# A memory-augmented attention block with a gated MLP on one core: beta loaded behind the transposing loads of the second x segment, its gating instructions moved behind it

## The chip, the cores and the metric

The kernel runs on one core of one Trainium2 chip. Its engines are TensorE (PE: matmuls; PEld: its weight loads), VectorE (DVE), ScalarE (ACT), GpSimd (POOL) and SyncE (SP), which issues most DMAs. The metric is the device time of one execution in microseconds, as the median of several runs; lower is better.

## The reference

The input x is 2048 tokens of 512 bf16 values. Two branches are computed from it and mixed per token by a sigmoid gate.

```python
x = A_x
g = _sigmoid((x * gate_w).sum(-1, keepdims=True))
a = _A_ref(x, A_wq, A_wk, A_wv, A_wo, A_beta)
b = _B_ref(x, B_w_gate, B_w_up, B_w_down)      # (gelu(x@w_gate) * (x@w_up)) @ w_down
return g * a + (1 - g) * b
```

Branch A is attention with 32 heads of width 16 in four segments of 512 tokens. Within a segment it is causal softmax attention; over the segments before, a linear memory (M, z) is read and then updated:

```python
g = _sigmoid(beta).reshape(1, H, 1, 1)
...
a_dot = jnp.einsum('bhqk,bhkd->bhqd', p, vs)
pq = phi(qs)
num = jnp.einsum('bhld,bhde->bhle', pq, M)
den = jnp.einsum('bhld,bhd->bhl', pq, z)[..., None] + 1e-06
o = g * (num / den) + (1.0 - g) * a_dot
```

So beta, 32 values, sets for each head how much comes from the memory and how much from the softmax.

## The kernel before

All work is cut into named tasks, each a short list of instructions on one engine. A long string, ORDER, written out by hand, lists every task once; walking through it, the program appends each task's instructions to its engine's queue. An engine works its queue strictly in that order. Semaphore waits are added where a task reads what another engine wrote, or writes what another engine still reads. The relative order of two tasks on different engines in the string has no effect of its own; the order of two tasks on one engine has.

A name carries the segment and the part. For segment 0: K0_t, Q0_t, V0_m are the projections, G0_f and U0_f the gate and up products of the MLP (14 tiles of 128 columns each), out0_q and wo0_q the output products, all on TensorE. Kev, Qev, Vev, Gev are the evictions of their PSUM results, on DVE or on ACT (`:d` or `:a` behind the name). TensorE's results go to four PSUM banks; the digit behind a TensorE task is the bank. A task that opens a bank waits until the eviction of the bank's former result is done.

The attention scores go a separate way. The four matmul groups of `st0_tA` to `st0_tE` (t is a group of 8 heads) fill a PSUM region of 2048 columns; `exp0_tX` on ACT turns it into one of ten probability tiles, pt; `msk0_tX` on GpSimd multiplies the blocks on the diagonal by a triangle, one instruction per block (one for A, two each for B to E). `pv0_1` on TensorE then takes the probabilities of head groups 0 and 1 times the values, group 0 first, key block by key block in the order 0, 1, 7, 2, 6, 3, 5, 4; blocks 1 and 7 lie in the tiles of part B. Each matmul waits for the masks of its own tile. GpSimd's queue has the masks of groups 0 and 1 in the order 0B, 0D, 0C, 0E, goa0, 0A, 1A, 1C, 1D, gfull, 1B. The results of pv are transposed on DVE (`tp0_...`) and scaled with gq (`pvp0_...`); the eviction order on DVE and the opening of banks on TensorE are again ORDER's.

The tasks of beta form a chain across the engines:

```python
one("betab", DVE, ...)   # 4 copies: ball -> betab, one row of 8 values for each of 4 partition groups
one("bexp", ACT, ...)    # gq = exp(betab); gfull = exp(-ball)
one("gqa", POOL, ...)    # gq = gq + 1
one("gqb", DVE, ...)     # gq = 1 / gq      (this is 1 - sigmoid(beta))
one("gfull", POOL, ...)  # gfull = gfull + 1
```

`ld_beta` (line 367) is the load ahead of it: 32 values broadcast to 128 partitions, 8 KB. gq is read by the pvp tasks, gfull by the memory reads from segment 1 on.

SP's queue before begins with: x0_0, wk1, x0_t2, x0_t3, wq0, wq1, gw, beta, wv, wg0 (waits until wq1 has landed), the four transposing loads x1_2, x1_1, x1_3, x1_0 of the second x segment, wu1 (waits for wg0), x2_0 (waits for wu1), then vsh0_21 and further loads.

Of the kernel before, what the change touches and what calls it, by code (L numbers as in the profile page):

```python
# [861 lines left out]
ld_x0_0 ld_wk1 ld_x0_1 warm1:0 ident xtr0_1 xev0_1:d xtr0_0 warm2 xev0_0:d vones0 masks ld_wk0 causal1 gwz ld_x0_t2  # L862
ld_x0_t3 ld_wq0 ld_wq1 ld_gw ld_beta causal0 consts K0_1a:1 K0_3a:2 K0_3b K0_2a:3 K0_0a:0 K0_2b K0_0b K0_1b K0_0c
K0_2c K0_3c K0_1c Kev0_0:d Kev0_2:d kpadb0_0 kpadb0_2 causal kpada0_0 Kev0_3:a Q0_0:0 Qev0_0:a Q0_1:3 st0_0A gwtr:2
Kev0_1:d gwev Q0_3:0 ld_wv ld_wg0 Qev0_1:d V0_1b:1 V0_3a:2 V0_3b:3 exp0_0A Qev0_3:d Vev0_3a:a Vev0_1b:a st0_0B
Vev0_3b:d kpada0_2 kpada0_1 V0_0b:0 V0_1a:2 V0_2a:1 Vev0_0b:d G0_6:3 Gev0_6:d Vev0_1a:d Vev0_2a:d exp0_0B st0_0C
exp0_0C Q0_2:0 G0_2:3 V0_2b:2 ld_x1_2 ld_x1_1 betab ld_x1_3 ld_x1_0 st0_0D Vev0_2b:a exp0_0D Gev0_2:d kpadb0_1
Qev0_2:d phka0_0 V1_2b:1 V0_0a:3 G1_6:2 V1_0b:0 Vev1_2b:d phka0_2 st0_0E Vev0_0a:d Vev1_0b:d G0_1:1 bexp Gev1_6:a
exp0_0E Gev0_1:d Q1_2:3 V1_3b:2 V1_3a:0 kpada0_3 Qev1_2:d Vev1_3a:d phkb0_2 phkc0_2 Vev1_3b:d st0_1A gz0 gqa exp0_1A
gr0 Q1_0:1 V1_0a:3 G1_5:0 Vev1_0a:d gqb Gev1_5:d st0_1B Q1_1:2 K1_0:3 exp0_1B phkb0_0 ld_wu1 ld_x2_0 G0_5:0 Qev1_0:d  # L870
kpadb0_3 vsh0_21 st0_1C exp0_1C Qev1_1:d ld_x2_1 ld_x2_3 ktr0_3 ld_wg1 Gev0_5:d V1_2a:1 K1_3:2 K1_1:0 vsh0_01
Vev1_2a:a vsh0_20 ld_x2_2 ktr0_2 vsh0_00 ld_wd1 st0_1D phkc0_0 Kev1_1:d kpada1_1 G0_4:1 G0_3:0 Gev0_4:d Kev1_0:d
Gev0_3:d Kev1_3:a ld_wd0 ld_wu0 ktr0_1 ktr0_0 vsh1_20 ld_wo V1_1a:2 Vev1_1a:d exp0_1D st0_2A exp0_2A msk0_0B msk0_0D
msk0_0C kpada1_0 msk0_0E goa0 gob0 msk0_0A msk0_1A msk0_1C msk0_1D gfull msk0_1B G0_0:1 Q1_3:3 G1_1:0 Qev1_3:d phqa1_0
st0_2B Gev0_0:d Gev1_1:a pv0_1:2301 exp0_2B tp0_d01 tp0_d00 pvp0_01 Q2_0:3 Qev2_0:d tp0_d11 st0_2C K1_2:2 Kev1_2:d
pvp0_00 tp0_d10 gelu0 G0_8:3 G0_13:1 gd0_13 G0_10:2 G0_11:0 G0_9:1 gd0_8 gd0_10 gd0_9 gd0_11 G0_12:3 G0_7:2 gd0_12
G1_2:1 U0_0:0 gd0_7 Gev1_2:d pvp0_11 h0_0 U0_13:3 U0_10:2 h0_10 Q2_1:1 Qev2_1:d exp0_2C st0_2D mz0:0 U0_7:2 U0_9:1
pvp0_10 h0_13 exp0_2D phqb1_0 st0_2E exp0_2E phka1_0 h0_7 mza0 h0_9 ota0_0 phqa1_2 kpadb1_0 G1_4:3 U0_1:2 h0_1
Gev1_4:a V1_1b:0 st0_3A G1_0:1 U0_5:3 Q2_2:2 exp0_3A Vev1_1b:a Gev1_0:a Qev2_2:a kpadb1_1 st0_3B exp0_3B U0_11:0
U0_4:1 U0_12:2 st0_3C phkb1_0 exp0_3C phqc1_0 kpada1_2 h0_4 h0_5 U0_6:1 U0_2:3 h0_11 h0_12 phqb1_2 h0_2 G1_3:0  # L880
Gev1_3:d h0_6 kpadb1_2 st0_3D phka1_2 U0_3:2 h0_3 U0_8:3 h0_8 Q2_3:0 Qev2_3:d exp0_3D phkb1_2 msk0_2A msk0_2B msk0_2C
msk0_3A msk0_2E msk0_2D msk0_3C goc0 msk0_3B st1_0A msk0_3D pv0_3:1230 exp1_0A st1_0B exp1_0B tp0_d20 tp0_d21 pvp0_20
tp0_d30 ota0_1 pvp0_21 tp0_d31 kpada1_3 out0_1_0:1 out0_1_1 out0_1_2 V2_0a:2 Vev2_0a:d G1_9:3 V2_1b:0 Vev2_1b:d
wev0_1:d st1_0C G1_8:2 G1_10:0 G1_11:1 gelu1 gd1_9 G1_7:3 gd1_8 gd1_10 gd1_7 gd1_11 G1_13:2 gd1_13 G1_12:0 gd1_12
phqc1_2 phkc1_0 mzq0 pvp0_31 pvp0_30 ota0_3 V2_0b:3 Vev2_0b:d ota0_2 V2_1a:1 Vev2_1a:d out0_0_0:2 out0_0_1 out0_0_2
nd1_0:0 ndp1_0 phkc1_2 exp1_0C st1_0D exp1_0D K2_0:3 K2_2:1 wev0_0:d Kev2_0:d Kev2_2:a K2_1:0 st1_0E Kev2_1:d U1_2:2
h1_2 wo0_1:1 nd1_3:3 nd1_1:0 exp1_0E st1_1A ld_x3_2 vsh1_00 vsh2_01 ktr1_1 ktr1_0 oev0_1 ndp1_1 wo0_0:2 oev0_0
kpada2_0 vsh1_21 out0_2_0:1 nd1_2:0 msk1_0C msk1_0A exp1_1A st1_1B exp1_1B msk1_0B gz1 msk1_0E msk1_1A msk1_0D msk1_1B
out0_2_1 wo0_2:2 ndp1_2 st1_1C exp1_1C nd1_5:0 out0_2_2 ndp1_3 wev0_2:a ndp1_5 out0_3_0:3 st1_1D nd1_4:0 out0_3_1
out0_3_2 ktr1_2 dma0 vsh1_01 otr1_3 ndp1_4 otr1_0 oev0_2 phka2_0 msk1_1C wev0_3:d ktr1_3 dma1 vsh2_00 otr1_1 ld_x3_1  # L890
ld_x3_0 ld_x3_3 exp1_1D st1_2A exp1_2A gr1 msk1_1D pv1_1:1023 st1_2B exp1_2B tp1_d01 tp1_d00 kpadb1_3 V2_2b:0
Vev2_2b:d K2_3:1 Kev2_3:a G2_3:0 pvp1_00 Gev2_3:d tp1_d10 st1_2C U1_8:1 G2_1:0 otr1_2 V2_3a:2 h1_8 Gev2_1:d Vev2_3a:d
kpadb2_0 kpadb2_1 exp1_2C st1_2D phkb2_0 exp1_2D G2_6:1 wo0_3:0 U1_3:2 pvp1_01 tp1_d11 Gev2_6:a h1_3 phka2_2 oev0_3
st1_2E U1_0:3 V2_3b:1 G2_0:2 Gev2_0:d h1_0 Vev2_3b:d exp1_2E phkb2_2 st1_3A mz1:0 G2_4:2 G2_5:3 pvp1_10 mza1 Gev2_5:d
exp1_3A st1_3B exp1_3B Gev2_4:d U1_11:1 G2_2:0 Gev2_2:d ota1_0 U1_13:3 h1_13 U1_10:2 h1_10 h1_11 G2_11:0 G2_10:3
pvp1_11 phkc2_0 phkc2_2 ota1_1 otm1_0 otm1_1 G2_12:2 G2_9:1 st1_3C gelu2 gd2_11 gd2_12 G2_7:0 G2_13:2 gd2_10 gd2_9
gd2_7 gd2_13 G2_8:3 gd2_8 U1_7:1 U2_9:0 K3_0:2 h1_7 U2_5:3 Q3_0:1 phqa2_0 h2_9 h2_5 Qev3_0:d Kev3_0:d exp1_3C st1_3D
exp1_3D U1_1:0 U2_12:3 msk1_3A msk1_2A msk1_3B U2_13:1 h2_12 h1_1 h2_13 kpada2_1 st2_0A U1_9:2 V2_2a:3 U2_7:0 msk1_2D
msk1_2B msk1_2E h1_9 Vev2_2a:d vsh2_20 dma2 dma3 ktr2_0 ktr2_2 vsh2_21 exp2_0A phqb2_0 msk1_3D msk1_2C msk1_3C st2_0B
h2_7 kpada2_2 pv1_3:1230 tp1_d21 exp2_0B tp1_d20 V3_1a:2 Vev3_1a:a st2_0C exp2_0C pvp1_21 tp1_d31 U1_6:1 Q3_1:2  # L900
V3_0a:0 st2_0D h1_6 pvp1_20 Vev3_0a:d Qev3_1:a V3_2b:1 U1_4:2 U1_5:0 exp2_0D st2_0E exp2_0E tp1_d30 phqc2_0 h1_5 h1_4
ota1_2 Vev3_2b:a U1_12:3 h1_12 pvp1_31 pvp1_30 out1_1_0:0 st2_1A V3_1b:2 out1_1_1 V3_3a:3 exp2_1A st2_1B msk2_0B
msk2_0D Vev3_3a:a exp2_1B out1_1_2 U2_4:1 msk2_0E goa1 gob1 kpadb2_3 kpada2_3 msk2_0C msk2_0A msk2_1A ota1_3 h2_4
otm1_2 otm1_3 K3_1:3 mzq1 Vev3_1b:a wev1_1:a st2_1C msk2_1B goc1 U2_1:2 Q3_3:1 V3_0b:0 Kev3_1:d kpada3_0 h2_1 Qev3_3:d
kpadb2_2 exp2_1C msk2_1C st2_1D V3_2a:3 U2_6:2 exp2_1D Vev3_2a:a wo1_1:1 Vev3_0b:d kpadb3_0 h2_6 oev1_1 st2_2A msk2_1D
pv2_1:0231 exp2_2A st2_2B exp2_2B tp2_d00 pvp2_00 phqa2_2 tp2_d01 tp2_d10 pvp2_10 pvp2_01 tp2_d11 out1_0_0:0 out1_0_1
st2_2C phqb2_2 out1_0_2 V3_3b:2 Vev3_3b:d wev1_0:d out1_3_0:3 phqc2_2 pvp2_11 exp2_2C st2_2D exp2_2D wo1_0:1 out1_3_1
st2_2E nd2_0:2 out1_2_0:0 out1_3_2 msk2_2C gz2 gr2 gz3 gr3 goa3 ndp2_0 gob3 oev1_0 msk2_2D goc3 goa2 gob2 exp2_2E
st2_3A exp2_3A msk2_3A msk2_2B wev1_3:d G3_4:2 nd2_2:1 out1_2_1 Gev3_4:a ndp2_2 st2_3B exp2_3B nd2_4:3 G3_1:1 Gev3_1:d
out1_2_2 nd2_1:2 st2_3C dma4 ktr2_1 vsh3_20 vsh3_01 ktr2_3 dma5 ndp2_4 ndp2_1 G3_3:1 wo1_3:3 exp2_3C Gev3_3:a K3_2:2  # L910
st2_3D wev1_2:a msk2_2A kpada3_1 oev1_3 Kev3_2:d nd2_5:1 nd2_3:3 G3_0:0 G3_5:2 ndp2_3 ndp2_5 Gev3_0:d msk2_3C msk2_2E
exp2_3D st3_0A exp3_0A goc2 msk2_3D msk2_3B G3_2:3 wo1_2:1 Gev3_2:d G3_6:0 Gev3_6:a Gev3_5:d oev1_2 ota2_0 st3_0B
pv2_3:3210 exp3_0B tp2_d20 tp2_d21 K3_3:3 Kev3_3:a pvp2_20 pvp2_21 U2_3:2 tp2_d30 h2_3 st3_0C U2_8:3 U2_0:1 tp2_d31
otr2_2 otr2_0 dma6 dma7 otr2_1 vsh3_00 otr2_3 vsh3_21 h2_0 ota2_1 G3_7:2 G3_12:0 G3_10:1 gelu3 gd3_7 h2_8 ota2_2
kpadb3_2 kpadb3_3 pvp2_30 pvp2_31 ota2_3 G3_8:3 gd3_10 gd3_12 gd3_8 G3_9:2 G3_11:1 gd3_11 gd3_9 G3_13:0 U2_11:3 Q3_2:1
U2_10:2 Qev3_2:d h2_10 gd3_13 U2_2:0 U3_13:1 exp3_0C st3_0D exp3_0D h2_2 h2_11 otm2_3 otm2_2 kpadb3_1 otm2_0 otm2_1
# [42 lines left out]
```

## Time and profile before

| | |
|---|---|
| runs | 263.14, 263.89, 518.72 us; median 263.89 |
| profiled execution | 264.53 us, of it 262.8 us span |
| TensorE busy | 257.9 us, 98% of the span |
| DVE, ACT, POOL busy | 75%, 77%, 38% |
| granted TensorE clock | 1.00 |
| DMA | 16.50 MB, most of it in the first 46 us |

The three runs are one execution each; the profiled execution is another one. The profile's timeline lists instructions by start, duration, engine, line and operation, with the tile written and the tiles read; `x8` means that neighbours of one kind were merged, and a bracket gives the idle time of the engine ahead of the instruction and what ended it. A line number is often that of a helper shared by many tasks; which task it is follows from its place in ORDER.

### The profile page before, as it was taken

Reading aid. Unit: us, or ns where it says so; the run is one execution under the profiler, and the core shown is the slowest. Engines: PE = TensorE matmul, PEld = TensorE weight load, DVE = VectorE, ACT = ScalarE, POOL = GpSimd, SP = SyncE. Lnnn points to the kernel's source line nnn. Section 1 sums busy time; section 2 is a strip of 40 time slices with the busy share of each in tenths; the row PEclk is TensorE's granted clock in tenths of the full one; section 3 lists DMA queues with packets and bytes.
Section 4 is the critical chain, followed back from the end, with each engine's and each line's share of the span. In section 5 each row is a group of like instructions: output and inputs, shape, how many; then the busy total and the mean of one; then the engine's idle time right before and its main releaser. Section 6 shows DMA issues by size and latency. Waiting matters only on the chain.

```text
span 262.8 us, 6704 instructions
## 1 busy us (share of the span) xinstructions
PE 257.9 (98%) x2849; PEld 122.5 (47%) x2849; DVE 197.4 (75%) x412; ACT 203.2 (77%) x171; POOL 99.1 (38%) x163
## 2 busy tenths in 40 slices
...
GB/s 186 244 160 144 163 278 275 93 2 1 5 28 2 61 43 39 91 75 2 2 0 71 35 0 2 2 41 61 68 79 0 2 1 22 3 0 42 62 42 80
DMA packets 31974, 16.50 MB, mean 63 GB/s; under 512 B 21576, under 2 KB 31944, under 8 KB 31944
## 3 DMA queue, kind: packets, MB, share of 16 engines
...
q8 instruction: 22, 0.36, 0.6%
q10 hardware_dynamic: 416, 0.39, 0.4%
...
## 4 chain that ended last, share of the span: by engine, by line
PE 92%; DMA 4%; SPq 1%; issue 0%; DVE 0%; DVEq 0%
PE psD L448 47%; PE psD L734 19%; PE psX L601 9%; PE psD L643 6%; PE psD L748 5%; PE psD L498 5%; DMA wg<-in_B_w_gate_dram 3%; PE psD L546 1%; DMA wq<-in_A_wq_dram 1%; SPq L361 1%; PE psD L576 1%; SPq L341 1%; DVE ost L752 0%; DVEq L817 0%
## 5 line engine op out<-in xcount | busy, mean ns | idle before, releaser
L608 ACT ACTIVATE pt<-psX 128x2048 bf16<-128x2048 f32 x72 | 135.1, 1877 | 29.5 <-PE psX L601 27.9
L614 POOL TENSOR_TENSOR pt<-pt,ctri 128x256 bf16<-128x256 bf16 x128 | 92.6, 734 | 128.3 <-ACT pt L608 123.8
L448 PE MATMUL psD<-xT,wu 128*128 128x512 bf16 x224 | 54.6, 380 | 0.0
L448 PE MATMUL psD<-xT,wg 128*128 128x512 bf16 x224 | 53.4, 380 | 1.1 <-DMA wg<-in_B_w_gate_dram 1.1
L734 PE MATMUL psD<-wd,gb 128*128 128x512 bf16 x224 | 53.2, 380 | 0.0
L719 DVE TENSOR_TENSOR gb<-psD,gb 128x512 bf16<-128x512 f32 x56 | 37.2, 681 | 10.8 <-PE psD L448 10.7
L448 PEld LDWEIGHTS psD<-xT,wg 128*128 128x128 bf16 x224 | 20.8, 98 | 25.8 <-issue 2.6
L734 PEld LDWEIGHTS psD<-wd,gb 128*128 128x128 bf16 x224 | 20.7, 98 | 24.3 <-issue 2.1
L448 PEld LDWEIGHTS psD<-xT,wu 128*128 128x128 bf16 x224 | 20.2, 98 | 24.7 <-issue 2.6
L601 PE MATMUL psX<-qT,kD 32*128 32x192 bf16 (+7 forms) x512 | 28.5, 287 | 0.0
L529 DVE STREAM_TRANSPOSE tT<-psD 128x512 f32<-128x512 f32 x32 | 21.7, 701 | 5.6 <-PE psD L643 5.1
L442 DVE CAST gb<-psD 128x512 bf16<-128x512 f32 x20 | 13.6, 689 | 13.7 <-PE psD L448 13.7
L601 PEld LDWEIGHTS psX<-qT,kD 32*128 32x128 bf16 x512 | 8.2, 92 | 25.1 <-ACT pt L608 13.4
L498 PE MATMUL psD<-wv,xT 128*128 128x257 bf16 (+1 forms) x128 | 18.2, 273 | 0.0
L752 DVE SCALAR_TENSOR_TENSOR ost<-psD,gtok,wds 128x512 bf16<-128x512 f32 (+1 forms) x17 | 11.9, 711 | 7.7 <-PE psD L748 7.6
L667 DVE SCALAR_TENSOR_TENSOR ob<-tT,gq,rc 128x256 bf16<-128x256 f32 x32 | 16.7, 522 | 1.1
L702 ACT ACTIVATE gb<-psD 128x512 bf16<-128x512 f32 x28 | 15.0, 594 | 3.3 <-PE psD L448 3.3
L643 PE MATMUL psD<-pt,vnat 64*17 64x192 bf16 (+7 forms) x512 | 17.1, 283 | 0.0
L643 PE MATMUL psD<-pt,vsh 64*17 64x192 bf16 (+7 forms) x512 | 17.1, 283 | 0.0
L448 PE MATMUL psD<-xT,wq 128*128 128x512 bf16 x64 | 16.3, 379 | 0.0
L748 PE MATMUL psD<-wo,oT 128*128 128x512 bf16 (+1 forms) x68 | 16.2, 367 | 0.0
L498 PEld LDWEIGHTS psD<-wv,xT 128*128 128x128 bf16 x128 | 11.8, 97 | 6.6 <-issue 1.4
...
## 6 DMA issues: line engine op xcount, KB each, us to landing
...
```

The lines of the kernel that those rows point to most:

```text
L448: one(name, PE, n * T_MM, [I(lambda e, i=i: e.matmul(BK[sl.i][:, :], lhs(i), rhs(i), start=(i == 0), stop=(i == n - 1)), reads(i), [bk(sl) ...
L498: one(f"V{s}_{m}{'ab'[hf]}", PE, 2 * T_MM, [I(lambda e, i=i, sl=sl, a=a, z=z, xs=xs: e.matmul(BK[sl.i][:, 0:z - a], xs(i), wv[:, i, a:z], ...
L529: one(f"tp{name}", DVE, 0.605, [I(lambda e, sl=sl, ti=ti: e.transpose(tT[ti][:, :], BK[sl.i][:, :]), [bk(sl)], [("tT", ti)])], bias=bias)
L601: ins.append(I(lambda e, t=t, kb=kb, ncol=ncol, c0=c0, g=g: e.matmul(XALL[:, g * 512 + c0:g * 512 + c0 + ncol], kD[(4 * s + t) % R_KD][32 ...
L608: one(f"exp{s}_{name}", ACT, 2048 * 0.000833 + 0.05, [I(lambda e: e.activation(pt[slot][:, :, :], xin, ACTF.Exp, scale=ATT_SCALE), [("X",) ...
L614: ins.append(I(lambda e, mv=mv: e.tensor_tensor(mv, mv, cm, ALU.mult), [("pt", slot), ("causal",)], [("pt", slot)]))
L643: ins.append(I(lambda e, kb=kb, slot=slot, c0=c0, n=n, g=g, r0=r0, sl=banks[j], va=va: e.matmul(BK[sl.i][32 * g:32 * g + 17, 64 * kb:512], ...
L667: I(lambda e, ti=ti, ri=ri, t=t, j=j, dst=dst: e.scalar_tensor_tensor(out=dst, in0=t_rows(ti), scalar=gq[:, 2 * t + j:2 * t + j + 1], in1= ...
L702: t = one(f"gd{s}_{ft}", ACT, 0.485, [I(lambda e, gi=gi, f=f, sl=sl: e.activation(gb[gi][:, f, :], BK[sl.i][:, :], ACTF.Gelu_apprx_tanh), ...
L719: one(f"h{s}_{ft}", DVE, 0.605, [I(lambda e, sl=sl, gi=gi, f=f: e.tensor_tensor(gb[gi][:, f, :], BK[sl.i][:, :], gb[gi][:, f, :], ALU.mult ...
L734: mm.append(I(lambda e, fb=fb, gi=gi, f=f, q=q, sl=sl: e.matmul(BK[sl.i][:, :], gb[gi][:, f, q], wd[:, fb, :], start=(fb == 0), stop=(fb = ...
L748: one(f"wo{s}_{qt}{sfx}", PE, 4 * T_MM * w / 512, [I(lambda e, kb=kb, q=q, so=so, c=c, w=w: e.matmul(BK[so.i][:, 0:w], oT[:, kb, q], wo[:, ...
```

## The change

Only the string ORDER is edited; the diff is long because its lines are wrapped anew. It holds the same 1019 words before and after. Five tasks stand elsewhere, with the neighbours that stay:

```diff
 ld_wq1 ld_gw
-ld_beta
 causal0 ...
 V0_2b:2 ld_x1_2 ld_x1_1
-betab
 ld_x1_3 ld_x1_0
+ld_beta
 st0_0D ...
 Vev1_0b:d G0_1:1
-bexp
 Gev1_6:a exp0_0E ...
 st0_1A gz0
-gqa
 exp0_1A gr0 Q1_0:1 V1_0a:3 G1_5:0 Vev1_0a:d
-gqb
 Gev1_5:d st0_1B ... G0_5:0 Qev1_0:d
+betab
 kpadb0_3 vsh0_21 st0_1C exp0_1C
+bexp
 Qev1_1:d
+gqa
 ld_x2_1 ld_x2_3
+gqb
 ktr0_3 ld_wg1 Gev0_5:d V1_2a:1 K1_3:2 K1_1:0 ...
```

Seen by engine: on SP, ld_beta goes from between gw and wv to between x1_0 and wu1. On DVE, betab goes from behind Vev0_2a to behind Qev1_0, and gqb from behind Vev1_0a to behind Qev1_1 and ahead of Gev0_5. On ACT, bexp goes from behind exp0_0D to behind exp0_1C. On GpSimd, gqa stays between gz0 and msk0_0B. TensorE's queue is the same.

More of the change, by code (lines that the diff above doesn't have):

```diff
@@ L861 @@
 ORDER = """
[L862 to L916, printed above, removed]
@@ L917 @@
-h3_13 phqa3_2 out2_1_0:2 out2_1_1 st3_0E exp3_0E mz2:0 U3_7:3 U3_1:1 kpada3_2 mza2 mzq2 h3_1 phqa3_0 h3_7 phqb3_2
-st3_1A U3_9:0 U3_3:1 out2_3_0:3 exp3_1A phqb3_0 h3_3 st3_1B exp3_1B out2_0_0:1 out2_1_2 msk3_0D msk3_0B st3_1C
-out2_0_1 out2_0_2 exp3_1C st3_1D exp3_1D phqc3_2 h3_9 wev2_1:d out2_3_1 wo2_1:0 msk3_0A msk3_1A oev2_1 kpada3_3
-phqc3_0 msk3_0E st3_2A U3_8:2 out2_3_2 U3_6:0 exp3_2A msk3_0C msk3_1C msk3_1B wev2_0:a wev2_3:a msk3_1D h3_8 h3_6
-st3_2B dma9 pv3_1:2130 tp3_d00 tp3_d01 U3_2:2 exp3_2B st3_2C exp3_2C pvp3_00 h3_2 tp3_d10 wo2_3:1 U3_0:2 U3_11:3
@@ L922 @@
-oev2_3 pvp3_01 h3_0 tp3_d11 st3_2D U3_12:1 U3_10:2 h3_11 h3_12 exp3_2D nd3_0:0 ndp3_0 h3_10 st3_2E U3_4:3 wo2_0:1
-nd3_2:0 nd3_1:2 h3_4 exp3_2E st3_3A exp3_3A out2_2_0:3 out2_2_1 st3_3B pvp3_11 ndp3_1 ndp3_2 nd3_3:2 U3_5:0 out2_2_2
-oev2_0 pvp3_10 nd3_5:1 msk3_2B msk3_2A msk3_2D msk3_2E msk3_3A ndp3_3 wev2_2:d h3_5 exp3_3B st3_3C exp3_3C wo2_2:2
-out3_1_0:3 st3_3D out3_1_1 nd3_4:0 out3_1_2 dma8 exp3_3D msk3_3B msk3_2C msk3_3C msk3_3D wev3_1:a ota3_0 ndp3_5 oev2_2
-ndp3_4 ota3_1 dma11 otr3_2 otr3_1 otr3_3 otr3_0 pv3_3:1203 tp3_d20 tp3_d21 pvp3_20 pvp3_21 tp3_d30 tp3_d31 ota3_2
@@ L927 @@
-pvp3_31 pvp3_30 otm3_1 otm3_0 ota3_3 out3_0_0:1 out3_2_0:2 out3_0_1 out3_2_1 out3_3_0:0 out3_0_2 out3_3_1 wev3_0:a
-otm3_2 otm3_3 wo3_0:3 dma10 oev3_0 dma12 wo3_1:1 out3_2_2 out3_3_2 wo3_2:3 oev3_1 wev3_2:a oev3_2 wo3_3b:1 dma13 dma14
-wev3_3:a oev3_3b dma15b wo3_3a:2 oev3_3a dma15a
+ld_x0_0 ld_wk1 ld_x0_1 warm1:0 ident xtr0_1 xev0_1:d xtr0_0 warm2 xev0_0:d vones0 masks ld_wk0 causal1 gwz ld_x0_t2 ld_x0_t3 ld_wq0 ld_wq1 ld_gw
+causal0 consts K0_1a:1 K0_3a:2 K0_3b K0_2a:3 K0_0a:0 K0_2b K0_0b K0_1b K0_0c K0_2c K0_3c K0_1c Kev0_0:d Kev0_2:d kpadb0_0 kpadb0_2 causal kpada0_0
@@ new lines @@
+Kev0_3:a Q0_0:0 Qev0_0:a Q0_1:3 st0_0A gwtr:2 Kev0_1:d gwev Q0_3:0 ld_wv ld_wg0 Qev0_1:d V0_1b:1 V0_3a:2 V0_3b:3 exp0_0A Qev0_3:d Vev0_3a:a Vev0_1b:a
+st0_0B Vev0_3b:d kpada0_2 kpada0_1 V0_0b:0 V0_1a:2 V0_2a:1 Vev0_0b:d G0_6:3 Gev0_6:d Vev0_1a:d Vev0_2a:d exp0_0B st0_0C exp0_0C Q0_2:0 G0_2:3 V0_2b:2
+ld_x1_2 ld_x1_1 ld_x1_3 ld_x1_0 ld_beta st0_0D Vev0_2b:a exp0_0D Gev0_2:d kpadb0_1 Qev0_2:d phka0_0 V1_2b:1 V0_0a:3 G1_6:2 V1_0b:0 Vev1_2b:d phka0_2
+st0_0E Vev0_0a:d Vev1_0b:d G0_1:1 Gev1_6:a exp0_0E Gev0_1:d Q1_2:3 V1_3b:2 V1_3a:0 kpada0_3 Qev1_2:d Vev1_3a:d phkb0_2 phkc0_2 Vev1_3b:d st0_1A gz0
@@ new lines @@
+exp0_1A gr0 Q1_0:1 V1_0a:3 G1_5:0 Vev1_0a:d Gev1_5:d st0_1B Q1_1:2 K1_0:3 exp0_1B phkb0_0 ld_wu1 ld_x2_0 G0_5:0 Qev1_0:d betab kpadb0_3 vsh0_21 st0_1C
+exp0_1C bexp Qev1_1:d gqa ld_x2_1 ld_x2_3 gqb ktr0_3 ld_wg1 Gev0_5:d V1_2a:1 K1_3:2 K1_1:0 vsh0_01 Vev1_2a:a vsh0_20 ld_x2_2 ktr0_2 vsh0_00 ld_wd1
+st0_1D phkc0_0 Kev1_1:d kpada1_1 G0_4:1 G0_3:0 Gev0_4:d Kev1_0:d Gev0_3:d Kev1_3:a ld_wd0 ld_wu0 ktr0_1 ktr0_0 vsh1_20 ld_wo V1_1a:2 Vev1_1a:d exp0_1D
+st0_2A exp0_2A msk0_0B msk0_0D msk0_0C kpada1_0 msk0_0E goa0 gob0 msk0_0A msk0_1A msk0_1C msk0_1D gfull msk0_1B G0_0:1 Q1_3:3 G1_1:0 Qev1_3:d phqa1_0
@@ new lines @@
+st0_2B Gev0_0:d Gev1_1:a pv0_1:2301 exp0_2B tp0_d01 tp0_d00 pvp0_01 Q2_0:3 Qev2_0:d tp0_d11 st0_2C K1_2:2 Kev1_2:d pvp0_00 tp0_d10 gelu0 G0_8:3
+G0_13:1 gd0_13 G0_10:2 G0_11:0 G0_9:1 gd0_8 gd0_10 gd0_9 gd0_11 G0_12:3 G0_7:2 gd0_12 G1_2:1 U0_0:0 gd0_7 Gev1_2:d pvp0_11 h0_0 U0_13:3 U0_10:2 h0_10
+Q2_1:1 Qev2_1:d exp0_2C st0_2D mz0:0 U0_7:2 U0_9:1 pvp0_10 h0_13 exp0_2D phqb1_0 st0_2E exp0_2E phka1_0 h0_7 mza0 h0_9 ota0_0 phqa1_2 kpadb1_0 G1_4:3
+U0_1:2 h0_1 Gev1_4:a V1_1b:0 st0_3A G1_0:1 U0_5:3 Q2_2:2 exp0_3A Vev1_1b:a Gev1_0:a Qev2_2:a kpadb1_1 st0_3B exp0_3B U0_11:0 U0_4:1 U0_12:2 st0_3C
@@ new lines @@
+phkb1_0 exp0_3C phqc1_0 kpada1_2 h0_4 h0_5 U0_6:1 U0_2:3 h0_11 h0_12 phqb1_2 h0_2 G1_3:0 Gev1_3:d h0_6 kpadb1_2 st0_3D phka1_2 U0_3:2 h0_3 U0_8:3 h0_8
+Q2_3:0 Qev2_3:d exp0_3D phkb1_2 msk0_2A msk0_2B msk0_2C msk0_3A msk0_2E msk0_2D msk0_3C goc0 msk0_3B st1_0A msk0_3D pv0_3:1230 exp1_0A st1_0B exp1_0B
+tp0_d20 tp0_d21 pvp0_20 tp0_d30 ota0_1 pvp0_21 tp0_d31 kpada1_3 out0_1_0:1 out0_1_1 out0_1_2 V2_0a:2 Vev2_0a:d G1_9:3 V2_1b:0 Vev2_1b:d wev0_1:d
+st1_0C G1_8:2 G1_10:0 G1_11:1 gelu1 gd1_9 G1_7:3 gd1_8 gd1_10 gd1_7 gd1_11 G1_13:2 gd1_13 G1_12:0 gd1_12 phqc1_2 phkc1_0 mzq0 pvp0_31 pvp0_30 ota0_3
@@ new lines @@
+V2_0b:3 Vev2_0b:d ota0_2 V2_1a:1 Vev2_1a:d out0_0_0:2 out0_0_1 out0_0_2 nd1_0:0 ndp1_0 phkc1_2 exp1_0C st1_0D exp1_0D K2_0:3 K2_2:1 wev0_0:d Kev2_0:d
+Kev2_2:a K2_1:0 st1_0E Kev2_1:d U1_2:2 h1_2 wo0_1:1 nd1_3:3 nd1_1:0 exp1_0E st1_1A ld_x3_2 vsh1_00 vsh2_01 ktr1_1 ktr1_0 oev0_1 ndp1_1 wo0_0:2 oev0_0
+kpada2_0 vsh1_21 out0_2_0:1 nd1_2:0 msk1_0C msk1_0A exp1_1A st1_1B exp1_1B msk1_0B gz1 msk1_0E msk1_1A msk1_0D msk1_1B out0_2_1 wo0_2:2 ndp1_2 st1_1C
+exp1_1C nd1_5:0 out0_2_2 ndp1_3 wev0_2:a ndp1_5 out0_3_0:3 st1_1D nd1_4:0 out0_3_1 out0_3_2 ktr1_2 dma0 vsh1_01 otr1_3 ndp1_4 otr1_0 oev0_2 phka2_0
```

31 lines of the change are left out of this document (added).

## Prediction

> **What bounds the kernel now.** I read the page's header first, then busy time by stretches, then the timeline engine by engine between 15 and 45 us, where the moved instructions stand. An order written by hand fixes each engine's queue, so what matters is which queue entry sits behind which.
>
> ```profile
> span 262.8 us, 6704 instructions
> PE 257.9 (98%) x2849; PEld 122.5 (47%) x2849; DVE 197.4 (75%) x412; ACT 203.2 (77%) x171; POOL 99.1 (38%) x163
> ```
>
> ```profile
> 32.60:41.65 9.05, 9.05 (x177) 4.30 (x176) 6.65 (x14) 7.42 (x7) 5.20 (x8) 1.00 1.02 301
> 41.65:259.00 217.35, 217.35 (x2402) 98.66 (x2403) 169.21 (x346) 175.21 (x144) 82.22 (x121) 1.00 0.17 36
> ```
>
> The second fence gives, behind each stretch, its length and the busy time of PE, PEld, DVE, ACT and POOL, the granted clock and the DMA share. TensorE is busy for all of 32.60 to 41.65 and all of 41.65 to 259.00. A microsecond that TensorE loses near 40 us has no later idle time to be won back in; it goes onto the end. GpSimd, with 38%, looks harmless on average, so the question is what it does in the one stage that the change touches.
>
> ```profile
> 30.95 0.40 PE L601 MATMUL psX<-qT,kD 32*128 32x384 bf16 x8
> 31.73 1.89 PE L448 MATMUL psD<-xT,wk 128*128 128x512 bf16 x8
> 39.17 0.40 PE L601 MATMUL psX<-qT,kD 32*128 32x448 bf16 x8
> 39.50 0.39 PE L643 MATMUL psD<-pt,vnat 64*17 64x512 bf16 x4
> 40.72 0.36 PE L643 MATMUL psD<-pt,vnat 64*17 64x448 bf16 x4
> 41.65 1.02 PE L448 MATMUL psD<-xT,wq 128*128 128x512 bf16 x4
> ```
>
> This is TensorE's line: scores st0_1C at 30.95, the projections K1_3 and K1_1 from 31.73, scores st0_2B at 39.17, then pv0_1 (probabilities times values for head groups 0 and 1) from 39.50, its second key block of group 1 at 40.72, and the next projection Q2_0 at 41.65.
>
> ```profile
> 22.18 0.25 POOL L778 TENSOR_SCALAR gq<-gq 128x8 f32<-128x8 f32 x1 [1.56 <-ACT gq L775]
> 22.40 6.50 POOL L614 TENSOR_TENSOR pt<-pt,ctri 128x256 bf16<-128x256 bf16 x8
> 28.86 0.22 POOL L432 TENSOR_SCALAR gr<-gr 128x4 f32<-128x4 f32 x1
> 29.05 1.34 POOL L614 TENSOR_TENSOR pt<-pt,ctri 128x256 bf16<-128x256 bf16 x2
> 35.95 1.42 POOL L614 TENSOR_TENSOR pt<-pt,ctri 128x256 bf16<-128x256 bf16 x2 [1.18 <-ACT pt L608]
> 37.34 0.34 POOL L781 TENSOR_SCALAR gfull<-gfull 128x32 f32<-128x32 f32 x1
> 37.64 0.67 POOL L614 TENSOR_TENSOR pt<-pt,ctri 128x256 bf16<-128x256 bf16 x1
> 38.39 0.67 POOL L614 TENSOR_TENSOR pt<-pt,ctri 128x256 bf16<-128x256 bf16 x1
> ```
>
> This is GpSimd's queue. gqa (L778) at 22.18 stands directly ahead of the first causal masks (L614). Sixteen masks must be done for pv0_1: eight from 22.40, two from 29.05, four for exp0_1C and exp0_1D, and the pair at 37.64 and 38.39, which ends at 39.06. TensorE arrives at pv0_1 at 39.50. So the masks have only a small lead there, and a long one only because the first eight were worked off from 22.40 on.
>
> **The change, part by part.**
>
> The gate chain is ld_beta (SP), betab (four copies, DVE), bexp (two activations, ACT), gqa (one instruction, POOL), gqb (one, DVE). The number of instructions is the same; each moves. In POOL's own queue gqa does not move at all: before and after, gz0, gqa, msk0_0B, msk0_0D and so on. What moves is the event that it waits for.
>
> ```profile
> 21.90 0.20 ACT L775 ACTIVATE gq<-betab 128x8 f32<-128x8 bf16 x1
> 22.12 0.59 ACT L441 ACTIVATE gb<-psD 128x512 bf16<-128x512 f32 x1
> 31.40 1.88 ACT L608 ACTIVATE pt<-psX 128x2048 bf16<-128x2048 f32 x1 [0.20 <-PE psX L601]
> 33.17 0.38 ACT L506 ACTIVATE vnat<-psD 128x256 bf16<-128x256 f32 x1
> ```
>
> ScalarE. bexp started at 21.90; the next instruction at 22.12, so it occupies 0.22 us. Its new place is behind exp0_1C (31.40) and ahead of Vev1_2a, which starts at 33.17. So bexp starts at 33.17. From bexp's start to the first mask the old rows give 22.40 - 21.90 = 0.50, so **the first mask starts at 33.67 instead of 22.40**, 11.27 late. Vev1_2a, Kev1_3 and exp0_1D come 0.22 later; TensorE is later than that there, as follows.
>
> GpSimd. From then on all its inputs but the last are ready and it works without a pause. Start to start, from the rows above: eight masks 28.86 - 22.40 = 6.46; goa0 0.19; two masks 1.34; two pairs at 37.34 - 35.95 = 1.39 each, 2.78; gfull 0.30; the last pair 38.39 + 0.67 - 37.64 = 1.42. Sum 12.49, end at 46.16. What other work does to a mask is seen here:
>
> ```profile
> 25.89 1.62 POOL L614 TENSOR_TENSOR pt<-pt,ctri 128x256 bf16<-128x256 bf16 x1
> 39.01 0.95 POOL L614 TENSOR_TENSOR pt<-pt,ctri 128x256 bf16<-128x256 bf16 x1
> ```
>
> ```profile
> 18.45 0.73 DVE L763 COPY betab<-omem 32x8 bf16<-32x8 bf16 x4
> 25.78 1.22 DVE L464 SCALAR_TENSOR_TENSOR phk<-kT,phk 128x1024 bf16<-128x1024 bf16 x1
> 27.64 0.19 DVE L779 RECIPROCAL gq<-gq 128x8 f32<-128x8 f32 x1
> 28.64 0.68 DVE L442 CAST qT<-psD 128x512 bf16<-128x512 f32 x1
> 31.06 0.69 DVE L442 CAST gb<-psD 128x512 bf16<-128x512 f32 x1 [0.60 <-PE psD L448]
> 31.67 1.22 DVE L464 SCALAR_TENSOR_TENSOR phk<-kT,phk 128x1024 bf16<-128x1024 bf16 x1
> 39.02 0.42 DVE L460 TENSOR_SCALAR phq<-qT 128x1024 bf16<-128x1024 bf16 x1
> 42.27 0.61 DVE L667 SCALAR_TENSOR_TENSOR ob<-tT,gq,rc 128x256 bf16<-128x256 f32 x1
> ```
>
> A mask takes 0.67 alone, 1.62 beside phkc0_2 (25.78) and 0.95 beside phqa1_0 (39.02). The 6.46 already holds one such phkc (0.95 extra). After the change phkc0_0 (31.67 before) falls into the mask run in its stead, since it stands behind gqb, and phqa1_0 falls into it too: 0.28 more, **end at 46.44**. Bounds: without any such meeting 0.95 less, 45.2; with both at their full length and pvp0_01 (42.27) also in the way, 1.22 - 0.95 + 0.42 - 0.28 + 0.61 = 1.0 more, 47.4. I stay at 46.44, the value of the rows. [...]
>
> VectorE. betab (0.73) leaves 18.45, where the next cast waited for TensorE anyway, and comes behind Qev1_0 (28.64): from 29.3 to 30.0; bexp wants it at 33.17, so it is covered. gqb is the worse move. It waits for gqa, 33.45 + 0.25 = 33.7, and queued behind it are Gev0_5 (31.06 before), phkc0_0, Kev1_1 and the rest. gqb ends near 33.95, Gev0_5 near 34.65. K1_1 writes the PSUM bank that Gev0_5 empties, so TensorE, done with K1_3 (the first four of the eight from 31.73) at 32.6, stands until about 34.75: a stall of 2.15. It is not added to the other; it delays TensorE's arrival at pv0_1 from 39.50 to 41.65, still ahead of the masks. gob0 (behind goa0, now near 40.1) and Qev1_3 end before TensorE needs the banks for pv0_1.
>
> TensorE. pv0_1 waits mask by mask. Group 0 needs the first nine (about 41.0 to 41.2), so it runs at 41.65. Group 1 needs the last pair from its second key block on. Before, that block began at 40.72 and Q2_0 at 41.65: 0.93 of work is left when the last mask lands. From a row of ACT releasing GpSimd (21.90 + 0.20 to 22.18) the hand-over is 0.08. Q2_0 starts at 46.44 + 0.08 + 0.93 = 47.45 instead of 41.65: **+5.80**. TensorE idles about 3.7 us inside pv0_1.
>
> SyncE and the DMA.
>
> ```profile
> 6.31 0.37 SPq L341 DMA_DIRECT2D omem<-in_A_beta_dram  x1
> 6.73 0.42 SPq L341 DMA_DIRECT2D wv<-in_A_wv_dram  x1
> 8.47 0.37 SPq L341 DMA_DIRECT2D wg<-in_B_w_gate_dram  x1
> 16.04 0.58 SPq L341 DMA_DIRECT2D wu<-in_B_w_up_dram  x1
> ```
>
> ```profile
> 16.12 1.02 PE L448 MATMUL psD<-xT,wg 128*128 128x512 bf16 x4 [1.09 <-DMA wg<-in_B_w_gate_dram]
> 8.00:9.00 1.00, 1.00 (x11) 0.80 (x9) 1.00 (x3) 0.49 (x1) 0.00 (x0) 1.00 0.26 77
> ```
>
> ld_beta leaves its place ahead of ld_wv, which issues 6.73 - 6.31 = 0.42 earlier, into a DMA that is only 0.26 busy from 8 to 9. ld_wg0 waits for wq1 and does not move, but its bytes queue behind wv. TensorE waits 1.09 for it. The gain is between 0 (wg0 not helped) and 0.42 (all of it); I take 0.3, nearer to the upper end because of that low DMA share. All later times, the masks' start among them, come earlier by it. At its new place ld_beta holds up ld_wu1 (16.04) and, through it, the x2 loads, vsh and wg1 by some 0.4; x2, wg1 and wu are first needed at 41.65 and later, so this is covered; bare it would cost 0.4.
>
> **Sum:** 5.80 - 0.3 = +5.5. The profiled execution took 264.53 (span 262.8 and 1.73 around it), giving 270.0. The median of the runs, 263.89, is 0.64 lower and would give 269.4. I name the middle, 269.7. About 2% is what a measurement of this kernel can tell from no change; that line lies 5.28 above the median, just under my sum.
>
> **Rivals.**
>
> The array comes back slow. After the 3.7 us pause inside pv0_1 TensorE might run at half its rate for a while. For it:
>
> ```profile
> 0.82 3.16 PE L382 MATMUL psD<-const-bfloat16-1.0 128*128 128x80 bf16 x45 [0.82 <-PEq L944]
> 5.25 3.65 PE L476 MATMUL psD<-xT,wk 128*128 128x256 bf16 x32
> ```
>
> At the start 45 matmuls of 80 columns take 3.16 / 45 = 70 ns each (0.88 ns a column), later ones of 256 columns 3.65 / 32 = 114 ns (0.45). If the first of these is a slow state that lasts at most until 4.6 (the later row starts at 5.25), for 3.8 us, and it comes back once, half of 3.8 is lost: +1.9, time 269.7 + 1.9 = 271.6. Against it: the granted clock reads 1.00 in every stretch, and the longest pause in this trace, 1.09, left the matmuls behind it at full rate; nothing here pauses for 3.7. [...] I give this rival 0.14: the start does show a slower rate, and no row shows it come back.
>
> Part of the stall is absorbed. While TensorE stands, exp0_2B and the group 0 transposes run ahead, so ACT and DVE start the next stage with a lead. Against it: TensorE had no idle time behind 41.65 for that lead to fill. If a fifth to two fifths were absorbed, +3.3 to +4.4, time 267.5 to 268.6, middle 268.1: 0.08.
>
> The stall at K1_1 adds to the other. If the masks also waited for work behind it, 5.5 + 2.15 gives 269.7 + 2.15 = 271.9: 0.03, since the masks' inputs are ready without it.
>
> Not slower. If GpSimd's masks do not stand behind gqa's wait, or gq is ready by 33.67 - 5.8 = 27.9, pv0_1 starts on time, and only the earlier wg0 is left: -0.3, at most the whole wait of -1.09, on 264.2 (the middle without the +5.5): 263.9, at best 263.1. That is the case too if the new order does not reach GpSimd's queue as I read it. What decides is whether the last mask ends before 40.6. Against it stands bexp behind exp0_1C, which no row puts before 33: 0.05.
>
> **How the numbers follow.** The forecast has 0.70; its own range, by the bounds on the masks (45.2 to 47.4) and on wg0 (0 to 0.42), is +4.1 to +6.8 on 264.2, 268.3 to 271.0. About two thirds of it lies above the 2% line: 0.46 slower and 0.24 within. The slow array and the added stall give 0.17 slower, absorption 0.08 within, the last rival 0.04 within and 0.01 faster. Slower 0.63, same 0.36, faster 0.01. The range is stretched at the top for the slow array and down a little for absorption: 267.9 to 272.0.
>
> **What would show it.** Right: gq's rows on ACT near 33, the first mask near 33.5, sixteen masks almost without a gap to about 46; K1_1 near 34.5; pv0_1 split, group 1 waiting for GpSimd; Q2_0 near 47.2; wg0's wait near 0.8; busy TensorE behind that as before. Wrong: masks starting before 30, Q2_0 before 46, a clock below 1.00 or 512-column matmuls spaced well over the present 0.22 us behind the pause, or ending times that drift from Q2_0's delay.

## The result, and the profile after

The changed kernel takes 270.85 us (median of 6 runs, 269.75 to 271.74) against 264.16 before: ratio 1.0259, interval 1.0227 to 1.0292. The profiled execution took 270.84, with a span of 269.1 instead of 262.8. It is slower, as forecast, and by 6.7 instead of 5.5 us. The ratio, here and below, compares runs within 1.5% of the fastest of their kernel, and so leaves out one run of the kernel before (518.72 us) and one with bexp earlier (271.31).

The head of the page of the changed kernel, and its row of granted clocks in 40 slices of 6.7 us:

```profile
span 269.1 us, 6670 instructions
PE 255.7 (95%) x2815; PEld 122.6 (46%) x2849; DVE 197.8 (74%) x412; ACT 203.5 (76%) x171; POOL 99.1 (37%) x163
...
PEclk9999998899999999999999999999999999999999
```

TensorE's share fell from 98% to 95%, and two slices, between 40 and 54 us, are no longer at full clock. Part of the fall is not real: 34 matmuls have no record in this trace (2815 against 2849 before), which leaves small gaps marked `issue`. GpSimd's busy time is the same 99.1. What changed is when it works. GpSimd's timeline:

```profile
32.37 0.25 POOL L778 TENSOR_SCALAR gq<-gq 128x8 f32<-128x8 f32 x1 [12.84 <-ACT gq L775]
32.59 6.62 POOL L614 TENSOR_TENSOR pt<-pt,ctri 128x256 bf16<-128x256 bf16 x8
39.17 0.22 POOL L432 TENSOR_SCALAR gr<-gr 128x4 f32<-128x4 f32 x1
39.36 4.22 POOL L614 TENSOR_TENSOR pt<-pt,ctri 128x256 bf16<-128x256 bf16 x6
43.55 0.47 POOL L781 TENSOR_SCALAR gfull<-gfull 128x32 f32<-128x32 f32 x1
43.98 3.41 POOL L614 TENSOR_TENSOR pt<-pt,ctri 128x256 bf16<-128x256 bf16 x5
```

GpSimd stands for 12.84 us in front of gqa, one instruction of 0.25, and the first mask starts at 32.59 instead of 22.40. The release is ScalarE's, behind exp0_1C:

```profile
30.32 1.88 ACT L608 ACTIVATE pt<-psX 128x2048 bf16<-128x2048 f32 x1 [0.20 <-PE psX L601]
32.09 0.20 ACT L775 ACTIVATE gq<-betab 128x8 f32<-128x8 bf16 x1
32.31 0.38 ACT L506 ACTIVATE vnat<-psD 128x256 bf16<-128x256 f32 x1
```

TensorE's timeline of the changed kernel, from the first wg product to the scores st0_2C:

```profile
15.03 1.02 PE L448 MATMUL psD<-xT,wg 128*128 128x512 bf16 x3
...
30.64 1.02 PE L448 MATMUL psD<-xT,wk 128*128 128x512 bf16 x4
33.47 1.04 PE L448 MATMUL psD<-xT,wk 128*128 128x512 bf16 x4 [1.80 <-DVE gb L442]
...
40.39 0.39 PE L643 MATMUL psD<-pt,vnat 64*17 64x512 bf16 x4
...
41.59 0.39 PE L643 MATMUL psD<-pt,vsh 64*17 64x512 bf16 x4
45.44 0.54 PE L643 MATMUL psD<-pt,vsh 64*17 64x448 bf16 x4 [3.47 <-POOL pt L614]
...
47.46 1.49 PE L448 MATMUL psD<-xT,wq 128*128 128x512 bf16 x3 [0.33 <-issue]
48.88 0.40 PE L601 MATMUL psX<-qT,kD 32*128 32x384 bf16 x8
```

Of before, the row to set beside the last one:

```profile
42.61 0.40 PE L601 MATMUL psX<-qT,kD 32*128 32x384 bf16 x8
```

There is no wait for wg0 at 15.03. K1_1 waits 1.80 for Gev0_5, which stands behind gqb. pv0_1 is split as foreseen: group 0 from 40.39, the first block of group 1 until 41.98, then 3.47 us for the last masks. And one thing the forecast had only as a rival: three Q2_0 matmuls (the first of the four has no record) take 1.49, where four took 1.02 before. The granted clock by microsecond (the third number from the end of each row) says why:

```profile
44.00:45.00 1.00, 0.00 (x0) 0.00 (x0) 0.00 (x0) 0.99 (x2) 0.92 (x3) 1.00 0.73 162
45.00:46.00 1.00, 0.56 (x24) 0.37 (x32) 0.00 (x0) 1.00 (x1) 1.00 (x3) 0.75 0.80 101
46.00:47.00 1.00, 1.00 (x50) 0.45 (x24) 0.00 (x0) 1.00 (x1) 0.92 (x3) 0.50 0.79 267
47.00:48.00 1.00, 0.67 (x10) 0.40 (x4) 0.00 (x0) 0.25 (x1) 0.40 (x1) 0.50 0.48 169
48.00:49.00 1.00, 1.00 (x7) 0.16 (x9) 0.02 (x1) 0.00 (x0) 0.00 (x0) 0.54 0.00 0
49.00:50.00 1.00, 1.00 (x12) 0.41 (x5) 1.00 (x2) 0.00 (x0) 0.00 (x0) 1.00 0.00 0
```

The clock is at one half from about 45.5 (0.75 means half of that microsecond) to about 48.9, the 3.4 us right behind the pause.

The account, in this one execution: st0_2C starts at 48.88 instead of 42.61, 6.27 late, and the span is 6.3 longer; nothing is won or lost behind it. The 6.27 is made of 45.44 - 40.72 = 4.72 for the second block of group 1, which already contains the earlier wg0 (16.12 - 15.03 = 1.09), and of (48.88 - 45.44) - (42.61 - 40.72) = 1.55 for the half clock. So the mask queue costs 5.81, wg0 gives 1.09 back, the clock takes 1.55.

The chain of work that ended last, between 32 and 50 us, tells the same: it leaves TensorE and runs along GpSimd.

```profile
33.33 2.38 POOL pt L614 x2
...
39.20 0.19 POOL gr L432
39.39 2.08 POOL pt L614 x3
...
43.58 0.44 POOL gfull L781
...
44.72 0.68 POOL pt L614
45.40 0.04 issue
45.44 1.68 PE psD L643 x56
```

### The profile page after: what moved, and what is told of

Its sections match the earlier page's. It is cut to its first block, busy times and chain, and to the rows that moved or that the text cites. A ratio compares the mean times of both kernels' runs of the same rounds, so it can differ in the third digit from the quotient of the medians.

```text
span 269.1 us, 6670 instructions
## 1 busy us (share of the span) xinstructions
PE 255.7 (95%) x2815; PEld 122.6 (46%) x2849; DVE 197.8 (74%) x412; ACT 203.5 (76%) x171; POOL 99.1 (37%) x163
## 4 chain that ended last, share of the span: by engine, by line
PE 85%; POOL 5%; ACT 3%; issue 3%; DVE 2%; DMA 2%; SPq 0%; DVEq 0%
PE psD L448 40%; PE psD L734 18%; PE psX L601 8%; PE psD L643 6%; PE psD L498 5%; PE psD L748 5%; POOL pt L614 4%; DMA wk<-in_A_wk_dram 2%; PE psD L546 1%; ACT gb L697 1%; ACT pt L608 1%; PE psD L476 1%; PE psD L576 1%; DVE tT L529 0%; DVE gb L719 0%
## 5 line engine op out<-in xcount | busy, mean ns | idle before, releaser
L448 PE MATMUL psD<-xT,wu 128*128 128x512 bf16 x214 | 52.7, 380 | 1.3 <-issue 1.1
L448 PE MATMUL psD<-xT,wg 128*128 128x512 bf16 x216 | 52.2, 379 | 0.8 <-issue 0.3
L734 PE MATMUL psD<-wd,gb 128*128 128x512 bf16 x217 | 51.8, 379 | 0.8 <-issue 0.5
L643 PE MATMUL psD<-pt,vsh 64*17 64x192 bf16 (+7 forms) x512 | 18.2, 290 | 3.5 <-POOL pt L614 3.5
L643 PE MATMUL psD<-pt,vnat 64*17 64x192 bf16 (+7 forms) x512 | 18.0, 290 | 0.0
L442 DVE CAST qT<-psD 128x512 bf16<-128x512 f32 x13 | 8.9, 684 | 8.2 <-PE psD L448 8.1
```

The lines of the kernel that those rows point to most:

```text
L442: (DVE, 0.60, [I(lambda e: e.tensor_copy(dst, src()), [bk(sl), *reads], writes)]),
L448: one(name, PE, n * T_MM, [I(lambda e, i=i: e.matmul(BK[sl.i][:, :], lhs(i), rhs(i), start=(i == 0), stop=(i == n - 1)), reads(i), [bk(sl) ...
L643: ins.append(I(lambda e, kb=kb, slot=slot, c0=c0, n=n, g=g, r0=r0, sl=banks[j], va=va: e.matmul(BK[sl.i][32 * g:32 * g + 17, 64 * kb:512], ...
L734: mm.append(I(lambda e, fb=fb, gi=gi, f=f, q=q, sl=sl: e.matmul(BK[sl.i][:, :], gb[gi][:, f, q], wd[:, fb, :], start=(fb == 0), stop=(fb = ...
```

## The experiments

The theory: the loss comes from gqa's late input, because gqa stands ahead of the masks in GpSimd's queue. The rivals: the late load of beta; VectorE's stall at gqb; a sum of stalls; for the excess over the forecast, the half clock.

**The load alone.** From the kernel before:

```diff
-ld_beta  (behind ld_gw)      -betab  (behind ld_x1_1)
+ld_beta betab                (behind ld_x1_0); bexp, gqa, gqb as before
```

> Only the load of beta moves (behind the x1 loads); betab stands right behind it, and bexp, gqa, gqb keep their old places. Mask-queue theory (gqa's late input holds up the causal masks behind it on GpSimd): nothing holds the masks, the first one starts near 21.5, pv0_1 starts near 38.4 without a pause, and only the vanished wait for wg0 (1.09) is left: about 263.0 us (262.4 to 263.8), against 264.2 before. Rival (the late landing of beta is itself the cost): betab stands until beta lands near 18 and the loss stays, about 270. Rival (the earlier wg0 was chance): 264.2.

Measured: 264.50 against 264.28, ratio 1.0013 (0.9997 to 1.0030). The late load costs nothing that these times show. GpSimd in this kernel:

```profile
21.24 0.49 POOL L778 TENSOR_SCALAR gq<-gq 128x8 f32<-128x8 f32 x1 [1.56 <-ACT gq L775]
21.70 6.39 POOL L614 TENSOR_TENSOR pt<-pt,ctri 128x256 bf16<-128x256 bf16 x8
```

The masks start at 21.70, as the theory has it. But the expected gain of 1.1 is not there in the times, although this kernel's own profile shows the wg products at 15.18; that execution was the fastest of twelve, 263.79. The repeats at the end return to this.

**The four instructions alone.** From the changed kernel:

```diff
+ld_beta  (back behind ld_gw)
-ld_beta  (behind ld_x1_0)
```

> Only the four gate tasks move; ld_beta keeps its old place between gw and wv. Mask-queue theory: the masks start near 33.7, Q2_0 near 47.4 plus the slow array: the wait for wg0 (1.09) is back, so 270.85 + 1.1 = about 271.9 us (271.0 to 272.8). Rival (the load's new place makes the loss): about 264.

Measured: 271.84, ratio 1.0283 (1.0265 to 1.0301). The whole loss is here. Masks from 33.37, and the pause as in the changed kernel:

```profile
33.37 6.61 POOL L614 TENSOR_TENSOR pt<-pt,ctri 128x256 bf16<-128x256 bf16 x8
46.22 0.55 PE L643 MATMUL psD<-pt,vsh 64*17 64x448 bf16 x4 [3.46 <-POOL pt L614]
```

**gqa and gqb out of the way.** From the changed kernel, with the load, betab and bexp as late as there:

```diff
-gqa  (ahead of the masks)    -gqb  (ahead of Gev0_5)
+gqa  (behind msk0_1D)        +gqb  (ahead of pvp0_01)
```

> The changed kernel with two words moved on: gqa behind msk0_1D on GpSimd, gqb just ahead of pvp0_01 on VectorE. Beta's load, betab and bexp stay late. Mask-queue theory: masks start near 21.5 as before, K1_1 and pv0_1 wait for nothing, the granted clock stays 1.00, about 263.0 us (262.3 to 263.8), a little under the kernel before. Rival (a late gq costs by itself, at the first pvp): pvp0_01 and the banks behind it are late, 265 or more.

Measured: 263.85, ratio 0.9986 (0.9975 to 0.9998).

```profile
20.26 5.81 POOL L614 TENSOR_TENSOR pt<-pt,ctri 128x256 bf16<-128x256 bf16 x8
...
37.16 0.29 POOL L778 TENSOR_SCALAR gq<-gq 128x8 f32<-128x8 f32 x1
```

Moving two words takes the whole loss away. A gqa that runs only at 37.16 costs nothing, since gq's first reader, pvp0_01, ran at 42.27 before. This is the one version below both kernels, by a margin that hardly clears its interval; the 1.1 below before that was expected did not come.

**gqb alone out of the way.** From the changed kernel:

```diff
-gqb  (ahead of Gev0_5)
+gqb  (ahead of pvp0_01)
```

> The changed kernel with gqb alone moved, to just ahead of pvp0_01; gqa still stands ahead of the masks. Mask-queue theory: the stall at K1_1 (1.8) goes, but the masks still start near 32.6 and pv0_1 still waits for the last one; phkc0_0 then runs before the masks, so their run is about 0.9 shorter and Q2_0 comes 0.9 earlier; the pause inside pv0_1 grows to about 4.5 and the clock drops again: about 269.9 us (269.2 to 270.7). Rival (the two stalls add up): the whole 1.8 to 2.2 goes, 268.6 to 269.0. Rival (VectorE's stall behind gqb is the cause): about 264.

Measured: 270.68, ratio 1.0230 (1.0214 to 1.0245), 0.2 below the changed kernel. TensorE's stall at K1_1, behind gqb, is therefore no part of the loss: it is gone, and the time is nearly the same. The eight masks take 5.62, 1.0 shorter, since phkc0_0 runs ahead of them. But TensorE now reaches pv0_1 before msk0_0A too, and waits twice:

```profile
33.61 5.62 POOL L614 TENSOR_TENSOR pt<-pt,ctri 128x256 bf16<-128x256 bf16 x8
40.11 0.39 PE L643 MATMUL psD<-pt,vnat 64*17 64x512 bf16 x4 [0.60 <-POOL pt L614]
45.47 0.55 PE L643 MATMUL psD<-pt,vsh 64*17 64x448 bf16 x4 [3.46 <-POOL pt L614]
43.00:44.00 1.00, 0.00 (x0) 0.00 (x0) 0.85 (x2) 0.99 (x2) 1.00 (x2) 0.53 1.06 382
49.00:50.00 1.00, 1.00 (x10) 0.30 (x11) 0.98 (x2) 0.00 (x0) 0.00 (x0) 0.55 1.01 357
```

The half clock lasts from about 43.1 to 49.9, twice as long as in the changed kernel. That took back most of what the shorter masks gave: the three runs with a mean clock of 0.986 or 0.987 took 270.68 to 271.25, the two with 0.994 took 269.87 and 270.08. So gqb's late place does cost about 1 us in another way, by putting phkc0_0 among the masks, and here the clock hid it.

**The pause filled.** From the changed kernel:

```diff
+warm3:2  (ahead of pv0_1): 16 matmuls of 512 columns into PSUM bank 2, result not read
```

> The changed kernel plus 16 idle matmuls of 512 columns (3.5 us at the present 0.216 us spacing) into a free PSUM bank, just ahead of pv0_1; their result is overwritten unread. TensorE then works nearly through the time in which it waited for the masks. Slow-array theory (about 1.5 of the loss is the halved clock behind the pause): the clock stays 1.00, group 1 of pv0_1 still starts near 45.4 but takes 0.93 instead of 1.7, about 269.3 us (268.8 to 269.9), although TensorE has 3.5 us more to do. Rival (the slower pv0_1 and Q2_0 have another cause): 270.8 or more. Rival (the wait is not on the masks): 270.85 + 3.5 = 274.3.

Measured: 270.07 (269.18 to 270.77), ratio 1.0223 (1.0203 to 1.0243). By the times this is 0.8 under the changed kernel, half of what was expected and outside the expected range, and the two intervals overlap. One of the five runs still had a mean clock of 0.994 (270.75); the four others took 269.18 to 270.77, against 269.75 for the one run of the changed kernel with a clock of 1.000. So the times do not settle what the half clock costs. The trace of one execution, whose line numbers are three higher here, shows it:

```profile
40.54 3.63 PE L385 MATMUL psD<-wq,const-bfloat16-1.0 128*128 128x512 bf16 x16
...
45.42 0.36 PE L646 MATMUL psD<-pt,vnat 64*17 64x448 bf16 x4
...
46.29 1.04 PE L451 MATMUL psD<-xT,wq 128*128 128x512 bf16 x4
47.26 0.40 PE L604 MATMUL psX<-qT,kD 32*128 32x384 bf16 x8
```

From group 1's second block to st0_2C it is 47.26 - 45.42 = 1.84, as before (1.89), not 3.44. The masks end where they ended, and 3.6 us more of work on TensorE costs nothing there. The span of this profile is 267.4, 1.7 below the changed kernel's.

**gqa on VectorE.** From the changed kernel:

```diff
-one("gqa", POOL, ...)
+one("gqa", DVE, ...)    # directly ahead of gqb
```

> The changed kernel with gqa executed on VectorE, directly ahead of gqb, instead of on GpSimd. GpSimd's masks no longer stand behind it; VectorE still stands until bexp is done near 32.3, and Gev0_5 and K1_1 behind it. Mask-queue theory: masks start near 20.5, pv0_1 waits for nothing, what is left is the bare stall at K1_1 of 1.8, less what the earlier wg0 gives on average (about 0.4): about 265.7 us (265.0 to 266.4), clock 1.00. Rival (VectorE's stall makes most of the loss): 269 or more.

Measured: 267.31, ratio 1.0118 (1.0097 to 1.0139), above the expected range, and far below the rival's 269.

```profile
20.45 5.82 POOL L614 TENSOR_TENSOR pt<-pt,ctri 128x256 bf16<-128x256 bf16 x8
34.76 1.04 PE L448 MATMUL psD<-xT,wk 128*128 128x512 bf16 x4 [2.14 <-DVE gb L442]
43.87 1.04 PE L448 MATMUL psD<-xT,wq 128*128 128x512 bf16 x4
```

With the masks free, K1_1's stall is bare and costs 43.87 - 41.65 = 2.22: in the changed kernel it was hidden in the wait for the masks. The 1.8 that I had used is the wait in the changed kernel; with gqa on VectorE it is 0.34 longer: from K1_3's start to K1_1's it is 3.17 (31.59 to 34.76) instead of 2.83 (30.64 to 33.47). That gqa and the hand-over to gqb take longer on VectorE would explain it, but was not shown. In three of the six runs the mean clock was 0.994 (267.58 to 268.04), in three 1.000 (266.24 to 267.04): about 1.15 more for those with the drop.

**bexp one place earlier.** From the changed kernel:

```diff
-bexp  (behind exp0_1C)
+bexp  (ahead of exp0_1C)
```

> The changed kernel with bexp one place earlier on ScalarE, directly ahead of exp0_1C instead of behind it. Mask-queue theory: the first mask starts 2.0 earlier, near 30.6, K1_1 hardly waits, pv0_1's group 1 starts near 43.4 after a pause of about 2.5; 2.0 less, and if the pause is then too short for the clock to drop, another 1.5 less: about 267.4 us (266.9 to 268.0); 268.9 if it drops all the same. Rival (the place of the load or of betab counts, not the masks' start): 270.8.

Measured: 269.26 (267.09 to 271.31), ratio 1.0176 (1.0147 to 1.0205): the case with the drop.

```profile
30.71 6.59 POOL L614 TENSOR_TENSOR pt<-pt,ctri 128x256 bf16<-128x256 bf16 x8
43.53 0.42 PE L643 MATMUL psD<-pt,vsh 64*17 64x448 bf16 x4 [3.46 <-POOL pt L614]
```

Masks and group 1 come 1.9 earlier, as foreseen. The pause did not shrink, because K1_1's stall went too and TensorE arrived earlier by the same amount. The one run of it with a mean clock of 1.000 took 267.09, near the 267.4 named for that case.

**Both kernels again.** Three repeats of the kernel before and one of the changed kernel, without an edit:

> The kernel before once more, unchanged, for a second look at when TensorE gets wg0 with beta's load ahead of wv. If the earlier wg0 came from moving the load: the wg matmuls start between 15.8 and 16.2, as in the two profiles so far with the load in its old place (16.12 and 15.82). If it is chance from run to run: anywhere from 15.0 to 16.1, as in the profiles with the load in its new place.

> As the first repeat of the kernel before: 15.8 to 16.2 if the load's place decides, 15.0 to 16.1 if chance does.

> As the first repeat of the kernel before: 15.8 to 16.2 if the load's place decides, 15.0 to 16.1 if chance does.

> The changed kernel once more, unchanged. Mask-queue theory: gq's first row near 32 to 33, group 1 of pv0_1 near 45.4 to 46.4, pause inside pv0_1 near 3.5; the clock at 0.50 for about 3 us behind it (in five of the six timed runs so far the mean clock was 0.992 to 0.994, in one 1.000); 269.7 to 271.8 us.

The first wg row of each, in this order:

```profile
16.12 1.02 PE L448 MATMUL psD<-xT,wg 128*128 128x512 bf16 x4 [0.77 <-DMA wg<-in_B_w_gate_dram]
16.12 1.02 PE L448 MATMUL psD<-xT,wg 128*128 128x512 bf16 x4 [0.58 <-DMA wg<-in_B_w_gate_dram]
15.97 1.02 PE L448 MATMUL psD<-xT,wg 128*128 128x512 bf16 x4 [0.41 <-DMA wg<-in_B_w_gate_dram]
15.91 1.02 PE L448 MATMUL psD<-xT,wg 128*128 128x512 bf16 x4 [0.98 <-DMA wg<-in_B_w_gate_dram]
```

With the load in its old place the wg products start at 16.12, 15.82, 16.12, 16.12 and 15.97 in five profiles, mean 16.03; in its new place at 15.03, 15.18, 15.79, 16.06, 15.18, 15.98, 15.23 and 15.91 in eight, mean 15.55. The three repeats of the kernel before came out where the load's place was expected to hold them, 15.8 to 16.2; in the new place the start is spread over 1 us, and the changed kernel itself shows both 15.03 and 15.91. So the new place allows an early start in some executions, 0.5 earlier on average in these few profiles and 1.1 at best. The wait for wg0 alone, as the brackets give it (none counted as 0), is 0.57 on average in the old place and 0.35 in the new: less than half of the 0.5. In the times of the load moved alone no gain shows; where it is lost stays open. The repeat of the changed kernel (271.65) had the same pause of 3.46 and the half clock behind it.

## Why the prediction was right, point by point

The mask queue: right in mechanism and size. From bexp's start to the first mask 0.50 was forecast and 32.59 - 32.09 = 0.50 measured; from the first mask to the resumption of group 1 the forecast was 46.52 - 33.67 = 12.85, measured 45.44 - 32.59 = 12.85. That the two agree to the last digit is luck: the 0.28 set aside for phqa1_0 and 0.04 of the hand-over were used up otherwise, for start to start the eight masks took 6.58 (6.46 forecast), the six behind goa0 4.19 (4.12), gfull 0.43 (0.30). The four instructions alone made all of the loss; gqa and gqb together out of the way took it away, and freeing the masks alone (gqa on VectorE) left K1_1's bare stall, 2.22, and in three of six runs a drop of the clock.

The stall at K1_1: right. It was forecast as 2.15, was 1.80, and lay inside the other wait. That it adds nothing was shown by taking it away (with gqb late the masks ran 1.0 shorter, the half clock twice as long, and the time was 0.2 lower), that it has a price when bare by freeing the masks (2.22).

That ld_beta's new place holds up ld_wu1 and the x2 loads at no cost: borne out, as the load alone left the time the same and TensorE waits for no load in its trace from 15 us on.

The earlier wg0, 0.3: in the profile of the changed kernel 1.09, over all profiles 0.5, in the times of the load alone nothing. The term was of the right order, and its spread from run to run was not in the forecast.

Q2_0 near 47.2 came true too, at about 47.1, but by two errors that cancel: the last mask ended at 45.40, 0.74 ahead of the forecast 46.14 (46.44 less the 0.3), mostly by the earlier wg0, and the work left behind it took about 1.7 instead of 0.93, by the half clock.

What failed is the choice among the cases: the half clock, given 0.14, is in every profile with a pause of about 3.46 us (the changed kernel and its repeat, the instructions alone, gqb late, bexp earlier) and, by their mean clock of 0.992 to 0.994, in five of the changed kernel's six runs. It cost 1.55 here, where the rival's price was 1.9. The argument against it, "the longest pause in this trace, 1.09, left the matmuls behind it at full rate", was no evidence about a pause three times as long. The row of the first matmuls was a hint and should have had more weight; that they were in the same state is not shown, since the granted clock reads 1.00 there and 0.50 behind the pause. In this execution wg0's gain, 0.79 more than forecast, paid for half of what the clock took. The other rivals fell: nothing behind the pause absorbed any of it (st0_2C 6.27 late, the span 6.3 longer), and the stalls do not add up.
